# 64-row last terms of two tiles in the two halves of TensorE's rows

## The chip, the cores and the metric

The kernel runs on one core of a Trainium2 chip. The metric is the device time of one execution in microseconds (us), the median of several runs. Beside the runs there is one profiled execution, whose trace tells each instruction's start and length; its span is the time from its first to its last instruction.

## The reference

Sequence length S = 2048, width D = 576, 32 heads of 18, all in float32.

```
xn  = layernorm(x)
qkv = xn @ wqkv                       # [2048, 3*576]
# per head: a query at position p sees the 8 positions p, p-2, ..., p-14
o   = softmax(q . k[window] * 18**-0.5) . v[window]
h   = max(xn @ w1, 0)                 # [2048, 4608]
out = x + o @ wo + h @ w2
```

## The kernel before

**Split numbers.** Each float32 operand is kept as a high part rounded to float32r, which TensorE multiplies in one pass, and a low part, the rest. A product is the sum of high by high, low by high and high by low. The contraction of 576 is four blocks of 128 rows and one of 64 (`DR`). In xT, block 4 ("mix") holds the high part of these 64 rows in partitions 0 to 63 and the low part in partitions 64 to 127; in w1, wq and wo the 64 rows are loaded twice, into both halves. `TERMS` (line 307) lists the 14 matmuls of one product: four of high by high, four of x low by w high, `(4, 4)`, which does both for the last 64 rows at once, and five of x by w low. The last of these, `(4, 9)`, is the 64-row block by w low; all 128 rows go through it, though only the upper 64 are of use.

**Phases, slots, steps.** Positions are taken in two phases (even and odd ones); each has eight row tiles `i` of 128 positions, or four blocks `tb` of 256. A slot is one (phase, chunk, tb, f): one h tile of 128 hidden units by 256 positions. There are 2 x 12 x 4 x 3 = 288 slots, and chunk c covers hidden units f = 0, 1, 2. The main loop (line 680) takes one step `n` per slot, and the order in which it issues is the order of each engine's queue:

1. `run_splits(n)`: weights that are due are split: `two` (line 136) makes the high part on ACT (line 137) and the low part on DVE (line 141). w1 is due 5 steps and w2 3 steps ahead of its slot's number, wq in the five steps ahead of its unit.
2. `h_mm(n + 2)`: 14 matmuls into a bank of the pool `ps_h`, which has two; then `h_out`: relu to hhi on ACT (line 500), and hlo on DVE (line 503). The hlo is the last reader of the bank.
3. What `todo` holds: `qkv_tile`, `wo_f`, `wo_b`, x loads, `make_xt` (five transposes, lines 274 and 275, and the splits of xT on ACT and DVE).
4. `o_mm(n)`: 12 matmuls of h by w2 into `ps_o`; after each third slot (f = 2) two adds into x on DVE (line 544).
5. What `todo_late` holds: attention's start, norms, `wo_a`, `wo_s`; then `run_bg`: attention runs on DVE as a queue of small pieces (`qk_mul` line 358, `qk_sum` line 361, `av_mul` line 388, `av_add` line 395 and the softmax between them). A piece is issued while the kernel's own count of DVE time, `t["dve"]`, is at most its count of PE time, `t["pe"]`, plus a margin of 3.0, 1.5 or 3.0 us.

qkv is done in four units of 8 heads in each phase. A unit has eight tiles, one a step, each 14 matmuls of 128x432 into a bank of `ps_m` (two banks), and three copies out on ACT (lines 327 to 329). The units begin at steps 7, 34, 61 and 88 of a phase, and wo at 123. After the unit's last tile ACT issues the halo's DMAs (line 333).

Of the kernel before, what the change touches and what calls it, by code (L numbers as in the profile page):

```python
# [10 lines left out]
F32 = mybir.dt.float32  # L11
F32R = mybir.dt.float32r
AF = mybir.ActivationFunctionType
# [4 lines left out]
P = 128  # L18
NPH = 2
NI = 8  # L20
NTB = 4
TBN = 256
W = 8
HG = 8
NU = 4
# [1 line left out]
LAG = 2  # L27
EPS = 1e-5

UNIT0, UNIT_STEP, WO_AT = 7, 27, 8  # L30
WO_STEPS = (0, 1, 3, 4, 6, 7, 9, 10)
HEADW = (-9, -8, -7, -6, -5, -4)
FIRST = 4

HEAD = (
# [12 lines left out]
def tile_body(ctx: ExitStack, tc: tile.TileContext, x, wqkv, wo, w1, w2, out):  # L48
    nc = tc.nc
# [3 lines left out]
    UD = HG * Dh  # L53
# [3 lines left out]
    DR = D - KT * P  # L57
# [5 lines left out]
    ctx.enter_context(tc.manual_schedule())  # L63
    pool = lambda name, bufs, **k: ctx.enter_context(tc.tile_pool(name=name, bufs=bufs, **k))
    consts = pool("consts", 1)
    xp = pool("xp", 11)
    xtp = pool("xtp", NTB)
    qop = pool("qop", 1)
    kp = pool("kp", 1)
# [4 lines left out]
    stp = pool("stp", 5)  # L74
    hp = pool("hp", LAG + 2)
    prp = pool("prp", 2)
    lgp = pool("lgp", 2)
    smp = pool("smp", 2)
    tmp = pool("tmp", 2)
    turned = pool("turned", 3, space=bass.MemoryType.DRAM)  # L80
# [1 line left out]
    ps_h = pool("ps_h", 2, space=PSUM)  # L82
    ps_m = pool("ps_m", 2, space=PSUM)
# [18 lines left out]
    t = {"pe": 0.0, "dve": 0.0}  # L102

    def mm(o, l, r, start, stop, n):
        nc.tensor.matmul(o, l, r, start=start, stop=stop)  # L105
        t["pe"] += n / 2400.0 + 0.002
# [5 lines left out]
    tasks = deque()  # L112
    staged = deque()
# [19 lines left out]
    by_pool = set()  # L133
# [10 lines left out]
    W1, W2, WQ, WO = {}, {}, {}, {}  # L144
# [76 lines left out]
    X, XT, XN, MR = {}, {}, {}, {}  # L221
# [39 lines left out]
            dve(600)  # L261
        XN[ph, i] = xn

    def transpose_split(src, hi, mix, lo, bank=None, parts=False):

        if bank is ps_o:
            po = ps_o.tile([P, 2, 512], F32, name="po")
            pa, pb = po[:, 0, :].rearrange("p (k c) -> p k c", k=KT), po[0:DR, 1, 0:P]
        else:
            pa = ps_m.tile([P, KT, P], F32, name="pm")  # L270
            pb = ps_h.tile([P, TBN], F32, name="ph") if bank is ps_h else ps_m.tile([P, P], F32, name="pm")
            pb = pb[0:DR, 0:P]
        for k in range(KT):
            nc.tensor.transpose(pa[:, k, :], src[:, k * P : (k + 1) * P], ident)  # L274
        nc.tensor.transpose(pb, src[:, KT * P : D], ident)
        t["pe"] += 5 * 0.06

        def high():
            nc.scalar.activation(hi, pa, AF.Copy)  # L279

        def low():
            nc.vector.tensor_tensor(lo, pa, f32(hi), op=ALU.subtract)
            dve(512)

        def last_high():
            nc.scalar.activation(mix[0:DR], pb, AF.Copy)

        def last_low():
            nc.vector.tensor_tensor(mix[DR:P], pb, f32(mix[0:DR]), op=ALU.subtract)
            dve(128)  # L290

        steps = high, low, last_high, last_low
        if not parts:
            for f in steps:
                f()
        return steps

    def make_xt(ph, i, bank=None, parts=False):
        tb, h = divmod(i, 2)
        if h == 0:  # L300
            XT[ph, tb] = xtp.tile([P, 9, TBN], F32R, name="xT")
        d = XT[ph, tb][:, :, h * P : (h + 1) * P]
        xn = XN.pop((ph, i))
        return transpose_split(xn, d[:, 0:4, :], d[:, 4, :], d[:, 5:9, :], bank, parts)


    TERMS = [(k, k) for k in range(KT)] + [(5 + k, k) for k in range(KT)] + [(4, 4)] + [(k, 5 + k) for k in range(5)]


    QO, KK, VV = {}, {}, {}  # L310

    def qkv_tile(ph, u, i):
        if u == 0 and i == 0:
            QO[ph] = qop.tile([P, NI, D], F32, name="qo")
        if i == 0:
            assert len(bg) < 38, len(bg)
            KK[ph, u] = kp.tile([P, W - 1 + NI, UD], F32, name="k")
            VV[ph, u] = vp.tile([P, W - 1 + NI, UD], F32, name="v")
            nc.gpsimd.memset(KK[ph, u][0:1, 0 : W - 1, :], 0.0)
            nc.gpsimd.memset(VV[ph, u][0:1, 0 : W - 1, :], 0.0)  # L320
        k, v, wq = KK[ph, u], VV[ph, u], WQ[ph, u]
        tb, h = divmod(i, 2)
        xt = XT[ph, tb]
        pq = ps_m.tile([P, 3, UD], F32, name="pm")
        for j, (a, b) in enumerate(TERMS):
            mm(pq, xt[:, a, h * P : (h + 1) * P], wq[:, b, :], j == 0, j == len(TERMS) - 1, 3 * UD)
        nc.scalar.activation(k[:, W - 1 + i, :], pq[:, 1, :], AF.Copy)  # L327
        nc.scalar.activation(v[:, W - 1 + i, :], pq[:, 2, :], AF.Copy)
        nc.scalar.activation(QO[ph][:, i, u * UD : (u + 1) * UD], pq[:, 0, :], AF.Copy)
        if i == NI - 1:  # L330
            for z in (k, v):
                for a, b in HALO:
                    nc.scalar.dma_start(z[a + 1 : b + 1, 0 : W - 1, :], z[a:b, NI : NI + W - 1, :])

    bg = deque()
# [141 lines left out]
    slots = [(ph, c, tb, f) for ph in range(NPH) for c in range(NCH) for tb in range(NTB) for f in range(C)]  # L477
    H, PO = {}, {}

    HP, HN = {}, {}  # L480

    def h_terms(n, terms, other=False):
        ph, c, tb, f = slots[n]
        w, xt = W1[ph, c, f], XT[ph, tb]
        if n not in HP:
            HP[n] = ps_m.tile([P, TBN], F32, name="pm") if other else ps_h.tile([P, TBN], F32, name="ph")
            HN[n] = 0
        for a, b in terms:
            wb = w[:, b // 5, (b % 5) * P : (b % 5 + 1) * P]
            HN[n] += 1  # L490
            mm(HP[n], wb, xt[:, a, :], HN[n] == 1, HN[n] == len(TERMS), TBN)

    def h_out(n, parts=False):
        pt = HP.pop(n)
        hi = hp.tile([P, TBN], F32R, name="hhi")
        lo = hp.tile([P, TBN], F32R, name="hlo")
        H[n] = (hi, lo)

        def high():
            nc.scalar.activation(hi, pt, AF.Relu)  # L500

        def low():
            nc.vector.scalar_tensor_tensor(lo, pt, 0.0, f32(hi), op0=ALU.max, op1=ALU.subtract)  # L503
            t["dve"] = max(t["dve"], t["pe"] + 0.6)
            dve(TBN)

        if not parts:
            high()
            low()
        return high, low  # L510

    def h_mm(n):
        h_terms(n, TERMS)
        h_out(n)

    def o_mm(n, out=True):
# [39 lines left out]
    todo = {}  # L556

    def at(n, f, *a):
        todo.setdefault(n, []).append((f, a))

    todo_late = {}

    def late(n, f, *a):
        todo_late.setdefault(n, []).append((f, a))
# [2 lines left out]
    for ph in range(NPH):  # L567
        b = ph * SPP
        for c in range(NCH):
            for f in range(C):  # L570
                s = b + c * SPC + f
                first = ph == c == 0
                plan.append((HEADW[f] if first else s - 5, w1_task, ((ph, c, f), c * C + f)))
                plan.append((HEADW[3 + f] if first else s - 3, w2_task, ((ph, c, f), c * C + f)))
        for u in range(NU):
            s = b + UNIT0 + u * UNIT_STEP
            plan.append((s - 5, wq_tasks, ((ph, u), u)))
            for i in range(NI):
                at(s + i, qkv_tile, ph, u, i)
            late(s + NI + 1, attention, ph, u)  # L580
        s = b + UNIT0 + NU * UNIT_STEP + WO_AT
        plan.append((s - 8, wo_tasks, (ph,)))
        for i in range(NI):
            z = s + WO_STEPS[i]
            late(z, wo_a, ph, i)
            at(z + 1, wo_f, ph, i)
            late(z + 2, wo_s, ph, i)
            at(z + 3, wo_b, ph, i)
            at(z + 3, done, ph, i)
        if ph + 1 < NPH:  # L590
            e = b + SPP - SPC
            for i in range(NI):
                z = e + 3 + 2 * i
                at(z - 6, load_x, ph + 1, i)
                late(z - 2, stats, ph + 1, i)
                late(z - 1, norm, ph + 1, i)
                at(z + 1, make_xt, ph + 1, i)
# [4 lines left out]
            f(step, *a)  # L602
    tasks = deque(sorted(tasks, key=lambda z: z[0]))

    by_pool.update((-9, -8, *range(UNIT0 - 5, UNIT0)))
    both, x_low, w_low, last = TERMS[0:4], TERMS[4:8], TERMS[9:13], [TERMS[8], TERMS[13]]
    load_x(0, 0, 2)
    load_x(0, 1)
# [9 lines left out]
    x0 = make_xt(0, 0, parts=True)  # L618
    x0[0]()
    run_splits(-9)  # L620
    x1 = make_xt(0, 1, bank=ps_o, parts=True)
# [57 lines left out]
    M = (3.0, 1.5, 3.0)  # L679
    for n in range(FIRST, len(slots)):  # L680
        run_splits(n)
        m = n + LAG
        if m < len(slots):
            h_mm(m)
        for f, a in todo.pop(n, []):
            f(*a)
        if n >= 0:
            o_mm(n)
        for f, a in todo_late.pop(n, []):
            f(*a)  # L690
        run_bg(M[slots[n][3] if n >= 0 else 0])
    assert not todo and not todo_late and not bg and not tasks and not staged


# [24 lines left out]
```

## Time and profile before

| | |
|---|---|
| median of 3 runs | 1180.94 us (1180.86 to 1181.31) |
| the profiled execution | 1181.42 us, its span 1179.7 us |
| PE busy | 1171.0 us, 8936 matmuls |
| h matmuls (ph<-xT,w1t 128x256) | 4018 records, 278 ns mean length |
| o matmuls (po<-w2t, 128x288) | 3456, 293 to 296 ns |
| qkv matmuls (pm<-wq,xT 128x432) | 896, 358 ns |
| DVE busy | 818.8 us |
| hlo (line 503) | 287, 421 ns mean |
| ACT busy | 301.9 us |
| granted TensorE clock | 1.00 |

PE is the row of matmuls, PEld that of weight loads, which run ahead of their matmuls; a matmul's length in the table reaches past the start of the next one, so what counts for time is the distance between starts. DVE is VectorE, ACT ScalarE. A line of the timeline gives start and length in us, engine, line, operation, what it writes and reads, shapes and how many are merged, and in brackets how long the engine was idle before and what ended that.

### The profile page before, as it was taken

Reading aid. Unit: us, or ns where it says so; the run is one execution under the profiler, and the core shown is the slowest. Engines: PE = TensorE matmul, PEld = TensorE weight load, DVE = VectorE, ACT = ScalarE, POOL = GpSimd, SP = SyncE. Lnnn points to the kernel's source line nnn. Section 1 sums busy time; section 2 is a strip of 40 time slices with the busy share of each in tenths; the row PEclk is TensorE's granted clock in tenths of the full one; section 3 lists DMA queues with packets and bytes.
Section 4 is the critical chain, followed back from the end, with each engine's and each line's share of the span. In section 5 each row is a group of like instructions: output and inputs, shape, how many; then the busy total and the mean of one; then the engine's idle time right before and its main releaser. Section 6 shows DMA issues by size and latency. Waiting matters only on the chain.

```text
span 1179.7 us, 21695 instructions
## 1 busy us (share of the span) xinstructions
PE 1171.0 (99%) x8936; PEld 1162.3 (99%) x8936; DVE 818.8 (69%) x1298; ACT 301.9 (26%) x738; POOL 47.5 (4%) x70
## 2 busy tenths in 40 slices
PE   8999999999999999999999999999999999999998
PEld 8999999999999999999999999999999999999998
DVE  7427875888687678877673288758777884887752
ACT  5412222131222222321233123121222322222210
POOL 3200000010000000000020000000100000000000
PEclk9999999999999999999999999999999999999999
DMA  5312121130321211355342113030302313113431
GB/s 182 97 34 76 55 61 56 38 108 1 99 58 46 74 48 42 94 129 134 107 148 66 46 53 88 27 83 23 96 22 79 79 34 89 54 30 99 110 99 61
DMA packets 137650, 86.15 MB, mean 73 GB/s; under 512 B 48864, under 2 KB 121312, under 8 KB 137552
## 3 DMA queue, kind: packets, MB, share of 16 engines
q1 hardware_dynamic: 134736, 76.28, 23.7%
q10 hardware_dynamic: 2816, 8.49, 2.5%
q8 instruction: 70, 1.15, 0.4%
q14 instruction: 28, 0.23, 0.1%
HBM read 66.58 MB, written 9.96 MB: 65 GB/s over the span
## 4 chain that ended last, share of the span: by engine, by line
PE 96%; DVE 1%; DMA 1%; ACT 0%; issue 0%; POOL 0%; SPq 0%; DVEq 0%; ACTq 0%; POOLq 0%
PE ph L105 38%; PE po L105 38%; PE pm L105 20%; PE pm L274 0%; DVE bst L239 0%; DMA xn<-turned 0%; DMA x<-in_x 0%; DMA st<-in_wqkv 0%; DMA turned<-tr 0%; DVE pr L395 0%; POOL rstd L245 0%; DVE w2t L141 0%; ACT xn L257 0%; DVE hlo L503 0%; DVE x L550 0%
## 5 line engine op out<-in xcount | busy, mean ns | idle before, releaser
L105 PE MATMUL ph<-xT,w1t 128*128 128x256 f32 x4018 | 509.3, 278 | 0.7 <-ACT xT L279 0.7
L105 PEld LDWEIGHTS ph<-xT,w1t 128*128 128x128 f32 x4018 | 489.1, 188 | 1.1 <-ACT xT L279 1.0
L105 PE MATMUL po<-w2t,hhi 128*128 128x288 f32 x2304 | 400.7, 296 | 0.0
L105 PEld LDWEIGHTS po<-w2t,hhi 128*128 128x128 f32 x2304 | 337.0, 188 | 1.0
L500 ACT ACTIVATE hhi<-ph 128x256 fp32r<-128x256 f32 x287 | 109.9, 383 | 583.4 <-PE ph L105 560.2
L105 PE MATMUL po<-w2t,hlo 128*128 128x288 f32 x1152 | 245.0, 293 | 0.0
L503 DVE SCALAR_TENSOR_TENSOR hlo<-ph,hhi 128x256 fp32r<-128x256 f32 x287 | 120.8, 421 | 169.2 <-ACT hhi L500 168.5
L544 DVE TENSOR_TENSOR x<-po,x 128x576 f32<-128x576 f32 x190 | 142.5, 756 | 67.2 <-PE po L105 64.1
L105 PE MATMUL pm<-wq,xT 128*128 128x432 f32 x896 | 185.5, 358 | 0.0
L105 PEld LDWEIGHTS po<-w2t,hlo 128*128 128x128 f32 x1152 | 183.8, 188 | 0.0
L105 PEld LDWEIGHTS pm<-wq,xT 128*128 128x128 f32 x896 | 163.8, 188 | 5.6
L358 DVE TENSOR_TENSOR pr<-qo,k 128x1152 f32<-128x1152 f32 x64 | 85.8, 1348 | 0.0
L361 DVE TENSOR_REDUCE lg<-pr 128x64 f32<-128x1152 f32 x64 | 84.9, 1342 | 0.0
L388 DVE TENSOR_TENSOR pr<-lg,v 128x1152 f32<-128x1152 f32 x64 | 84.6, 1348 | 0.2
L141 DVE TENSOR_TENSOR w2t<-st,w2t 128x576 fp32r<-128x576 f32 x72 | 54.3, 754 | 40.4 <-ACT w2t L137 40.2
L395 DVE TENSOR_TENSOR pr<-pr 128x288 f32<-128x288 f32 (+1 forms) x128 | 70.4, 598 | 0.1
L141 DVE TENSOR_TENSOR w1t<-st,w1t 128x640 fp32r<-128x640 f32 x70 | 57.3, 818 | 12.1 <-ACT w1t L137 12.0
L137 ACT ACTIVATE w2t<-st 128x576 fp32r<-128x576 f32 x72 | 49.3, 685 | 55.1 <-PE po L105 46.5
L327 ACT ACTIVATE k<-pm 128x144 f32<-128x144 f32 x64 | 18.6, 291 | 146.5 <-PE pm L105 146.5
L137 ACT ACTIVATE w1t<-st 128x640 fp32r<-128x640 f32 x72 | 52.9, 735 | 2.5 <-DMA st<-in_w 2.3
L364 POOL TENSOR_SCALAR_AFFINE_SELECT lg<-lg 1x512 f32<-1x512 f32 x8 | 9.4, 1172 | 836.7 <-DVE lg L361 836.7
L105 PE MATMUL pm<-wq,oT 128*128 128x288 f32 x224 | 35.2, 296 | 0.8 <-ACT oT L451 0.8
(71 smaller groups left out, 444.2 us busy)
## 6 DMA issues: line engine op xcount, KB each, us to landing
st<-in_w SPq DMA_DIRECT2D x72, 288.0 KB, 3.0
st<-in_w SPq DMA_DIRECT2D x72, 256.0 KB, 3.1
st<-in_wqkv SPq DMA_DIRECT2D x32, 216.0 KB, 3.1
turned<-tr SPq DMA_DIRECT2D x64, 80.0 KB, 2.2
xn<-turned SPq DMA_DIRECT2D x16, 320.0 KB, 3.3
st<-in_w SPq DMA_DIRECT2D x144, 32.0 KB, 2.8
x<-in_x SPq DMA_DIRECT2D x15, 288.0 KB, 4.4
out<-x SPq DMA_DIRECT2D x14, 288.0 KB, 2.2
```

The costliest lines, as they stand in the source:

```text
L105: nc.tensor.matmul(o, l, r, start=start, stop=stop)
L137: nc.scalar.activation(hi, src, AF.Copy)
L141: nc.vector.tensor_tensor(lo, src, f32(hi), op=ALU.subtract)
L327: nc.scalar.activation(k[:, W - 1 + i, :], pq[:, 1, :], AF.Copy)
L358: nc.vector.tensor_tensor(pr[i], q, window(k, i), op=ALU.mult)
L361: nc.vector.tensor_reduce(lg[:, i], pr.pop(i).rearrange(heads, d=Dh), axis=AX.X, op=ALU.add)
L364: nc.gpsimd.affine_select(out=z, in_=z, pattern=[[1, NI], [1, W], [0, HG]], compare_op=ALU.is_ge, fill=-1e9 / scale, base=1 - W, channel_m ...
L388: nc.vector.tensor_tensor(pr[i].rearrange(heads, d=Dh), e, window(v, i).rearrange(heads, d=Dh), op=ALU.mult)
L395: nc.vector.tensor_tensor(o, z[:, 0:n], z[:, n : 2 * n], op=ALU.add)
L500: nc.scalar.activation(hi, pt, AF.Relu)
L503: nc.vector.scalar_tensor_tensor(lo, pt, 0.0, f32(hi), op0=ALU.max, op1=ALU.subtract)
L544: nc.vector.tensor_tensor(acc, PO[k][:, :, 0:D2], acc, op=ALU.add)
```

## The change

From step 8 on, at each even step `h_pair` issues the `(4, 9)` terms of the two next slots ahead of everything else of TensorE in that step. Each is a matmul of 64 rows: the first slot's reads partitions 0 to 63 of w1's low part and of mix, the second slot's partitions 64 to 127, where w1 has the same rows and where xT has a tenth block, the "twin", with the same high part. They open the two banks of `ps_h`, and each slot's other 13 terms add to them in its own step. Likewise `qkv_pair` opens the two banks of `ps_m` for two qkv tiles. The twin is one more copy on ACT for each row tile. Unit starts become even steps, the last x tile of the second phase is prepared a step earlier, and to make room `xp` has 10 buffers instead of 11 and `lgp` one instead of two; x loads for the second phase come 4 steps ahead instead of 6 from the third tile on.

```diff
-UNIT0, UNIT_STEP, WO_AT = 7, 27, 8
+UNITS, WO_AT = (8, 34, 62, 88), 123
+PAIRED = 8
...
-    xp = pool("xp", 11)
+    xp = pool("xp", 10)
-    lgp = pool("lgp", 2)
+    lgp = pool("lgp", 1)
...
         def last_high():
             nc.scalar.activation(mix[0:DR], pb, AF.Copy)
+            nc.scalar.activation(twin[DR:P], pb, AF.Copy)
...
-            XT[ph, tb] = xtp.tile([P, 9, TBN], F32R, name="xT")
+            XT[ph, tb] = xtp.tile([P, 10, TBN], F32R, name="xT")
...
+    def pair(o0, o1, x0, x1, w0, w1, n, weights_move):
+        for o, x, w, rows in ((o0, x0[0:DR, 4], w0[0:DR], 0), (o1, x1[DR:P, 9], w1[DR:P], 1)):
+            nc.tensor.matmul(o, *((x, w) if weights_move else (w, x)), start=True, stop=False)
+        t["pe"] += n / 2400.0 + 0.002
...
+    def qkv_pair(ph, u, i):
+        xt, w = XT[ph, i // 2], WQ[ph, u][:, 9, :]
+        a, b = PQ[i], PQ[i + 1] = [ps_m.tile([P, 3, UD], F32, name="pm") for _ in range(2)]
+        pair(a, b, xt[:, :, 0:P], xt[:, :, P:TBN], w, w, 3 * UD, True)
...
-        pq = ps_m.tile([P, 3, UD], F32, name="pm")
-        for j, (a, b) in enumerate(TERMS):
-            mm(pq, xt[:, a, h * P : (h + 1) * P], wq[:, b, :], j == 0, j == len(TERMS) - 1, 3 * UD)
+        pq = PQ.pop(i)
+        for a, b in TERMS[:-1]:
+            mm(pq, xt[:, a, h * P : (h + 1) * P], wq[:, b, :], False, (a, b) == TERMS[-2], 3 * UD)
...
+    def h_pair(n):
+        o, x, w = [], [], []
+        for m in (n, n + 1):
+            ph, c, tb, f = slots[m]
+            HP[m] = ps_h.tile([P, TBN], F32, name="ph")
+            HN[m] = 1
+            x.append(XT[ph, tb])
+            w.append(W1[ph, c, f][:, 1, 4 * P : 5 * P])
+            o.append(HP[m])
+        pair(*o, *x, *w, TBN, False)
...
     def h_mm(n):
-        h_terms(n, TERMS)
+        h_terms(n, TERMS[:-1] if n in HP else TERMS)
         h_out(n)
...
-            s = b + UNIT0 + u * UNIT_STEP
+            s = b + UNITS[u]
...
+                if i % 2 == 0:
+                    begin.setdefault(s + i, []).append((qkv_pair, (ph, u, i)))
...
-                at(z - 6, load_x, ph + 1, i)
+                at(z - (6 if i < 2 else 4), load_x, ph + 1, i)
+                z -= i == NI - 1
...
         m = n + LAG
         if m < len(slots):
+            if n >= PAIRED and n % 2 == 0:
+                h_pair(m)
+            for f, a in begin.pop(n, []):
+                f(*a)
             h_mm(m)
```

More of the change, by code (lines that the diff above doesn't have):

```diff
@@ L262, in norm, with transpose_split @@
         XN[ph, i] = xn
-    def transpose_split(src, hi, mix, lo, bank=None, parts=False):
+    def transpose_split(src, hi, mix, lo, twin, bank=None, parts=False):
         if bank is ps_o:
@@ L300, in make_xt @@
         if h == 0:
-            XT[ph, tb] = xtp.tile([P, 9, TBN], F32R, name="xT")
+            XT[ph, tb] = xtp.tile([P, 10, TBN], F32R, name="xT")
         d = XT[ph, tb][:, :, h * P : (h + 1) * P]
         xn = XN.pop((ph, i))
-        return transpose_split(xn, d[:, 0:4, :], d[:, 4, :], d[:, 5:9, :], bank, parts)
+        return transpose_split(xn, d[:, 0:4, :], d[:, 4, :], d[:, 5:9, :], d[:, 9, :], bank, parts)
     TERMS = [(k, k) for k in range(KT)] + [(5 + k, k) for k in range(KT)] + [(4, 4)] + [(k, 5 + k) for k in range(5)]
+    def pair(o0, o1, x0, x1, w0, w1, n, weights_move):
+        for o, x, w, rows in ((o0, x0[0:DR, 4], w0[0:DR], 0), (o1, x1[DR:P, 9], w1[DR:P], 1)):
+            nc.tensor.matmul(o, *((x, w) if weights_move else (w, x)), start=True, stop=False)
+        t["pe"] += n / 2400.0 + 0.002
     QO, KK, VV = {}, {}, {}
+    PQ = {}
+    def qkv_pair(ph, u, i):
+        xt, w = XT[ph, i // 2], WQ[ph, u][:, 9, :]
+        a, b = PQ[i], PQ[i + 1] = [ps_m.tile([P, 3, UD], F32, name="pm") for _ in range(2)]
+        pair(a, b, xt[:, :, 0:P], xt[:, :, P:TBN], w, w, 3 * UD, True)
     def qkv_tile(ph, u, i):
@@ L559, in at @@
         todo.setdefault(n, []).append((f, a))
-    todo_late = {}
+    todo_late, begin = {}, {}
     def late(n, f, *a):
@@ L575, in tile_body @@
         for u in range(NU):
-            s = b + UNIT0 + u * UNIT_STEP
+            s = b + UNITS[u]
             plan.append((s - 5, wq_tasks, ((ph, u), u)))
             for i in range(NI):
+                if i % 2 == 0:
+                    begin.setdefault(s + i, []).append((qkv_pair, (ph, u, i)))
                 at(s + i, qkv_tile, ph, u, i)
             late(s + NI + 1, attention, ph, u)
-        s = b + UNIT0 + NU * UNIT_STEP + WO_AT
+        s = b + WO_AT
         plan.append((s - 8, wo_tasks, (ph,)))
@@ L603, in tile_body @@
     tasks = deque(sorted(tasks, key=lambda z: z[0]))
-    by_pool.update((-9, -8, *range(UNIT0 - 5, UNIT0)))
+    by_pool.update((-9, -8, *range(UNITS[0] - 5, UNITS[0])))
     both, x_low, w_low, last = TERMS[0:4], TERMS[4:8], TERMS[9:13], [TERMS[8], TERMS[13]]
@@ L691, in tile_body @@
         run_bg(M[slots[n][3] if n >= 0 else 0])
-    assert not todo and not todo_late and not bg and not tasks and not staged
+    assert not begin and not todo and not todo_late and not bg and not tasks and not staged
 def kernel(**inputs):
```

## The prediction

> **What bounds the kernel now.** I read the page first: busy shares, then the chain that ended last.
>
> ```profile
> PE 1171.0 (99%) x8936; PEld 1162.3 (99%) x8936; DVE 818.8 (69%) x1298; ACT 301.9 (26%) x738; POOL 47.5 (4%) x70
> ...
> PE 96%; DVE 1%; DMA 1%; ACT 0%; issue 0%; POOL 0%; SPq 0%; DVEq 0%; ACTq 0%; POOLq 0%
> ```
>
> TensorE is the bound: the chain is 96% PE. Every matmul taken off shortens the end, and every wait put in front of PE lengthens it, one for one. DVE at 69% looks like slack, so I asked the view of waits how VectorE stands to PE at the one instruction that frees an h bank, the hlo of line 503.
>
> ```profile
> DVE hlo L503 <- ACT hhi L500: 168.5, 135, 5.5
> ```
>
> There are 288 hlo, and DVE waited for the relu (hhi) before 135 of them. The others began when DVE was done with older work: DVE is behind there. Today that costs nothing, since ps_h has two banks and a tile's bank is wanted again only two slots on. How late it is I read from the timeline, here slot 48's start (adds, attention, splits, hlo of slot 47):
>
> ```profile
> 204.24 1.55 DVE L544 TENSOR_TENSOR x<-po,x 128x576 f32<-128x576 f32 x2
> ...
> 205.71 1.35 DVE L358 TENSOR_TENSOR pr<-qo,k 128x1152 f32<-128x1152 f32 x1
> ...
> 206.64 0.38 ACT L500 ACTIVATE hhi<-ph 128x256 fp32r<-128x256 f32 x1 [1.62 <-PE ph L105]
> ...
> 206.97 0.75 DVE L141 TENSOR_TENSOR w2t<-st,w2t 128x576 fp32r<-128x576 f32 x1
> ...
> 207.64 0.82 DVE L141 TENSOR_TENSOR w1t<-st,w1t 128x640 fp32r<-128x640 f32 x1
> ...
> 208.03 0.98 PE L105 MATMUL ph<-xT,w1t 128*128 128x256 f32 x7
> ...
> 208.38 0.42 DVE L503 SCALAR_TENSOR_TENSOR hlo<-ph,hhi 128x256 fp32r<-128x256 f32 x1
> ```
>
> Slot 48's matmuls start at 208.03, and slot 47's hlo ends at 208.79, 0.76 us later. The relu was done at 207.02; the two weight splits and an attention piece stood ahead on DVE.
>
> **Part 1: matmuls taken away.** Starts in the trace give the cadence: h 113 to 119 ns a matmul (14 in 1.61 us), o 132, qkv 196. The change pairs slots 10 to 287, 139 pairs, and 64 qkv tiles, 32 pairs. Each pair swaps two full matmuls for two of 64 rows; if these ran as one, h would save 139 x 0.11 = 15.3 us and qkv 32 x 0.19 = 6.1 us, 21.4 us in all. The other end is nothing saved. No row has two matmuls side by side, but one shows what a weight load costs by itself, a matmul that PE had to wait for:
>
> ```profile
> 1093.20 0.19 PEld L105 LDWEIGHTS pm<-wq,oT 128*128 128x128 f32 x1 [1.03 <-ACT oT L451]
> 1093.20 0.41 PE L105 MATMUL pm<-wq,oT 128*128 128x288 f32 x1 [0.83 <-ACT oT L451]
> ```
>
> It took 0.41 us where its like take 0.29 to 0.30, and its successor began 241 ns after it instead of 132. So a load of 128 columns is 0.107 us, hidden only under the matmul before it, and h's 113 ns is just that. A pair still has two such loads, and nothing in the trace shows two loads at once. I take loads one after another, matmuls side by side. With 0 at the end of the last o matmul, the first load has 132 to hide in and is done at -25, the second at 82, the next full matmul's at 189, which then starts at about 195: 33 ns saved of 228. With a qkv pair behind, loads end at 82, 189 and 296, and the last qkv matmul ends at 296 + 196 = 492 against 620: 128 ns saved. 107 x 0.033 + 32 x 0.128 = 7.6 us.
>
> **Part 2: going into half rows and back.** 139 bursts, 278 changes. The nearest row is the 64-column transpose of line 275 among full matmuls: from its start to the second full matmul behind it 229 ns passed, where 109 + 118 = 227 would at an even cadence; with an o matmul behind it, 4 or 5 ns were lost. Its 16 cases would make 278 x 2 to 5 ns, 1.0 us. Below nothing it cannot be. The other end is under C.
>
> **Part 3: the new wait.** The pair at an even step opens both banks, so its second matmul needs the hlo of the slot just before, which PE used to need one slot later. PE's order of the changed program has that wait: the second matmul of line 315 waits for DVE. Behind it in PE's queue stands everything: thirteen terms of the slot, qkv, and o, so nothing covers it. I measured at every even slot of the trace, as above, how long after its first matmul the hlo before it ended. In the first half (us): 24: 0.76, 34: 1.91, 36: 2.64, 48: 0.76, 60: 1.27, 84: 0.76, 88: 1.13, 90: 1.25, 96: 1.01, 108: 0.76, 116: 0.29, 118: 1.01, 120: 0.83, 144: 0.62, together 15.0. The second half repeats them without the last, 14.4. I leave out 18, 72 and 216 (0.24, 1.59, 1.60): there the relu was late behind the halo's DMAs on ACT, and units now end at odd steps, so the late relu belongs to an even slot. All 27 waits in full: 29.4 us; if one wait in a cluster (34/36, 88/90, 116 to 120) absorbs the next, 21.1. Each wait also exposes a load, 0.107, and the hand-over, 0.03: 2.7 to 3.8. Low end 24, high end 33, and up to 3 more because PE arrives sooner where pairs save. I take 30. A cluster pays more than its maximum: ahead of slot 35's hlo stand two adds (0.76), the maximum (1.16), and wq, w2t and w1t splits (0.60, 0.75, 0.82), with the hlo 5.3 us less 0.08 for each overlap, against some 4.0 us that PE has from when the first add can start; a second wait of about 1 us survives one at 34.
>
> The qkv pair opens both pm banks and needs wq's last split at once. The banks: three copies on ACT (0.29, 0.29, 0.30) after the last tile lie under the 1.59 us of o matmuls; without that cover 0.9 us a pair. The split stands on DVE ahead of the odd hlo that the h pair has just waited for: no wait of its own.
>
> The order of DVE's queue in the changed program keeps this: ahead of slot 47's hlo it has the same adds, piece and splits.
>
> **Part 4: the rest.** The twin copies are 16 more activations like line 286's, 0.26 us each, on an engine at 26%; only the first two lie on the start: 0.3 us. One lg buffer costs nothing, as DVE works its units in order. Ten x buffers make the third x load wait for an output (2.2 us to landing) and then 4.4 us, under more than two steps of 3.2: nothing; without that cover, about 1 us once. No DMA is added; units and the last xT a step apart from before put no work on PE.
>
> **Sum.** +30 - 7.6 + 1.0 + 0.3 = +23.7 us. The profiled execution was 1181.42 us (span 1179.7), 0.5 over the median of 1180.94; on the median, 1204.6. Its own range, with waits from 24 to 36 and pairs saving 9 to nothing: 1196 to 1218.
>
> **The rivals.**
>
> A, the sum above: 0.42.
>
> B, the halves run side by side, loads too. For it: nothing in the order forbids it, and the two write different banks. Against: the 0.107 us loads never overlap in this trace. Gain 21.4, waits 33 as PE comes sooner: +12, about 1193 (1184 to 1196). [...] 0.23.
>
> C, each change of form empties the array. Then the next load isn't hidden (0.107) and, at worst, the last matmul runs out first: it took 276 ns at a cadence of 113, another 0.163. 278 times 0.107 to 0.27 is 30 to 75 us. Less 21.4 plus 30 of waits: 1219 to 1265, likelier at the low end, 1230, as line 275's row shows nothing of it. That row speaks against C, but it cuts columns, not rows. [...] 0.30.
>
> D, the other side: not slower. run_bg gives DVE as much as PE's estimate allows, and that now falls by 0.109 us a pair; where an attention piece of 1.35 us slips behind the odd hlo, a wait of 0.76 to 1.27 is gone. It decides where waits fall under the gain: below 21.4 in B's case, so a third or more of the 27 places must clear. With half cleared, 14 - 21.4 = -7, 1174. Against it: the order holds as many pieces there as before. 0.05.
>
> **Numbers.** A measurement of this kernel can tell about 0.2%, 2.4 us, from no change. Only D gains that much, 0.04; its rest and B's edge lie within it, 0.02; slower 0.94. The range runs from 1190 (B's middle and up) to 1240 (C's low half); outside lie D, B's low tail and C's high part, about 0.18.
>
> **What would show it.** Right: PE idle of some 30 us in front of ph at line 315, ended by DVE hlo, about once in each twelve slots and more where splits of wq fall; idle of PE elsewhere as before; DVE's busy time unchanged. For A, the pair's second matmul about 0.1 us after the first; for B, a few ns; for C, a gap of 0.1 us or more on both sides of each pair. Wrong: no idle at line 315 (D), or PE's stretches without waits longer than before (C).

## The result, and the profile after

The changed kernel takes 1246.33 us (1244.82 to 1247.52, four runs) against 1180.90: a ratio of 1.0553, interval [1.0534, 1.0571], 65 us slower. The forecast was slower, 1204.6, with a range to 1240; the time lies 6 us above it.

The page of the kernel after, busy shares and the chain that ended last:

```profile
span 1244.5 us, 21715 instructions
...
PE 1217.8 (98%) x8936; PEld 1160.5 (93%) x8936; DVE 821.0 (66%) x1297; ACT 307.2 (25%) x754; POOL 50.0 (4%) x71
...
PE 82%; DVE 10%; issue 3%; DMA 2%; ACT 1%; SPq 1%; POOL 0%; DVEq 0%; ACTq 0%; POOLq 0%
```

DVE has come into the chain with 10% (1% before), and "issue", time in which an engine waits for nothing that the profile shows, with 3%. DVE's own busy time is what it was (818.8 before). The view of waits, lines of the pairs alone (us in total, times, longest):

```profile
PEld ph L315 <- DVE hlo L529: 25.2, 38, 1.6
PEld ph L315 <- issue: 20.7, 127, 0.2
...
PE ph L315 <- DVE hlo L529: 18.0, 28, 1.4
```

Two different things stand in front of line 315: a few long waits for hlo, and 127 short ones, 0.16 us each, that no semaphore ends. The timeline around one pair without a wait for hlo:

```profile
235.68 0.43 PE L106 MATMUL po<-w2t,hlo 128*128 128x288 f32 x2
236.03 0.19 PEld L315 LDWEIGHTS ph<-xT,w1t 64*128 64x128 f32 x2 [0.16 <-issue]
236.04 0.38 PE L315 MATMUL ph<-xT,w1t 64*128 64x256 f32 x2
236.35 0.54 PEld L106 LDWEIGHTS ph<-xT,w1t 128*128 128x128 f32 x4
236.35 0.62 PE L106 MATMUL ph<-xT,w1t 128*128 128x256 f32 x3
```

The two halves and their two loads start together (236.04 for both; 3 ns apart in the records). But the last o matmul began at 235.81, and the loads of the halves only at 236.03, 0.22 us later, where a load otherwise starts 3 ns after the matmul before it. On the other side the next full load waits until 236.35. So at each change of form no load runs ahead of its matmul, and PE stands for about 0.09 us besides: in front 0.22 us pass between the starts instead of 0.13, and behind 0.31, where an exposed load (0.107) and a matmul (0.113) make 0.22.

Call the half-row matmuls that follow one another without a full one between them a burst. Taken over all 139 bursts, from the start of the last o matmul to that of the second full h matmul, against the cadence of before: 283 ns more for a burst with an h pair alone, 80 more with a qkv pair behind it, 107 x 0.283 + 32 x 0.080 = 33 us. On top, the second half started late in 33 bursts, 28.9 us in all. Here is the one at slot 48, whose lateness the prediction had shown:

```profile
214.79 0.82 DVE L142 TENSOR_TENSOR w1t<-st,w1t 128x640 fp32r<-128x640 f32 x1
...
215.16 0.38 PE L315 MATMUL ph<-xT,w1t 64*128 64x256 f32 x1
...
215.53 0.42 DVE L529 SCALAR_TENSOR_TENSOR hlo<-ph,hhi 128x256 fp32r<-128x256 f32 x1
...
216.00 0.38 PE L315 MATMUL ph<-xT,w1t 64*128 64x256 f32 x1 [0.46 <-DVE hlo L529]
```

The first half goes at 215.16, the second when hlo has ended, at 216.00: 0.84 us. Together 62 of the 64.8 us by which the span has grown. Of the rest, 1.7 us is a stretch at a clock of 0.50 (last section), and 0.6 us falls behind the last matmul. What is left, about 1 us, fits what lies further behind the bursts with a qkv pair: over two whole steps such a burst costs 0.11 to 0.18 us more than before, not 0.08. Why is open.

### The profile page after: what moved, and what is told of

It reads as the page before. It is cut to its first block, busy times and chain, and to the rows that moved or that the text cites. A ratio compares the mean times of both kernels' runs of the same rounds, so it can differ in the third digit from the quotient of the medians.

```text
span 1244.5 us, 21715 instructions
## 1 busy us (share of the span) xinstructions
PE 1217.8 (98%) x8936; PEld 1160.5 (93%) x8936; DVE 821.0 (66%) x1297; ACT 307.2 (25%) x754; POOL 50.0 (4%) x71
## 4 chain that ended last, share of the span: by engine, by line
PE 82%; DVE 10%; issue 3%; DMA 2%; ACT 1%; SPq 1%; POOL 0%; DVEq 0%; ACTq 0%; POOLq 0%
PE ph L106 31%; PE po L106 30%; PE pm L106 17%; PE ph L315 3%; DMA st<-in_w 2%; DVE lg L376 1%; DVE w1t L142 1%; DVE w2t L142 1%; DVE hlo L529 1%; DVE pr L373 1%; DVE m L385 1%; PE pm L315 1%; DVE wq L142 0%; DVE x L570 0%; DVE pr L403 0%
## 5 line engine op out<-in xcount | busy, mean ns | idle before, releaser
L106 PE MATMUL ph<-xT,w1t 128*128 128x256 f32 x3740 | 493.6, 282 | 0.7 <-ACT xT L280 0.7
L106 PEld LDWEIGHTS ph<-xT,w1t 128*128 128x128 f32 x3740 | 455.2, 188 | 21.7 <-issue 6.8
L106 PE MATMUL pm<-wq,xT 128*128 128x432 f32 x832 | 174.4, 360 | 0.0
L106 PEld LDWEIGHTS pm<-wq,xT 128*128 128x128 f32 x832 | 152.7, 189 | 5.5
L315 PE MATMUL ph<-xT,w1t 64*128 64x256 f32 x278 | 64.4, 381 | 18.0 <-DVE hlo L529 18.0
L315 PEld LDWEIGHTS ph<-xT,w1t 64*128 64x128 f32 x278 | 31.2, 183 | 46.2 <-DVE hlo L529 25.2
```

The lines of the kernel that those rows point to most:

```text
L315: nc.tensor.matmul(o, *((x, w) if weights_move else (w, x)), start=True, stop=False)
```

## The experiments

Theory T: each change between full and half rows has a price (a load that cannot be hidden, 0.107 us, and 0.09 us for which PE stands, as around the pair above), the halves themselves run side by side (3 ns between their starts), and the waits for hlo, 28.9 us, come on top.

**Waits without half rows.** The order is kept; both matmuls of a pair go through all rows.

```diff
-((o0, x0[0:DR, 4], w0[0:DR], 0), (o1, x1[DR:P, 9], w1[DR:P], 1))
+((o0, x0[:, 4], w0, 0), (o1, x1[:, 4], w1, 1))
```

> The changed kernel with its order kept, but both matmuls of a pair go through all 128 rows, as the term did before; no half-row form is left. Theory T: the loss has two parts, about 29 us of waits for the odd hlo in front of the pairs, and a price for every change between full and half rows (0.107 us of exposed weight load and 0.09 us of running empty); then only the waits are left: 1208 to 1214 us, and 220 to 230 ns from pair to next full matmul vanish. Rival R1: the time around the pairs is lost by the order itself (PE's queue held at the pair, banks opened early), not by the form: 1235 to 1250.

Measured 1216.57 us, ratio 1.0299 [1.0269, 1.0329]: 35.3 us more than before, 2.6 us above the expected range and far from R1. The timeline of slot 48:

```profile
212.00 0.42 PE L106 MATMUL po<-w2t,hlo 128*128 128x288 f32 x2
212.26 0.28 PE L315 MATMUL ph<-xT,w1t 128*128 128x256 f32 x1
213.19 0.39 PE L315 MATMUL ph<-xT,w1t 128*128 128x256 f32 x1 [0.65 <-DVE hlo L529]
213.41 0.75 PE L106 MATMUL ph<-xT,w1t 128*128 128x256 f32 x5
```

The pair's first matmul follows o at the old distance, and the second's wait is there. 34 bursts lost 34.0 us, the other 105 together 0.6. They lose more than in the changed kernel (28.9) mostly because each wait also exposes a load (3.6 us), which there is already counted with the change of form; the lateness alone is 30.4 us.

**Half rows without pairs or waits.** The kernel before; in `h_terms`:

```diff
+            r = 64 if (a, b) == TERMS[-1] else P
-            mm(HP[n], wb, xt[:, a, :], HN[n] == 1, HN[n] == len(TERMS), TBN)
+            mm(HP[n], wb[0:r], xt[0:r, a, :], HN[n] == 1, HN[n] == len(TERMS), TBN)
```

> The kernel before, with one edit: the last term of each h tile takes 64 rows (upper half) in its old place, 288 lone half-row matmuls, no pair and no early bank. T: two changes of form each, 2 x 0.198 us, nothing saved: 288 x 0.396 = 114 us, 1290 to 1298, and no wait for hlo. R1: the form costs nothing, 1179 to 1184.

Measured 1291.94 us, ratio 1.0937 [1.0905, 1.0969]: 110.7 us over before, 0.384 us for each of 288. It is the price of the form alone, two changes each: 0.19 us a change. The by-form view of PEld has the part that stands in front (the last number is PEld's idle time before):

```profile
L105 PEld LDWEIGHTS ph<-xT,w1t 64*128 64x128 f32 x287 | 52.5, 183 | 36.3
```

That two matmuls add to the same bank is not what costs. In this run the half writes the bank of the matmul before it (206 ns between the starts instead of 113), and the matmul behind it writes another bank (310 ns, and 239 instead of 133 to the next). In the changed kernel it is the other way round, with much the same losses (225 instead of 131 in front, 311 and 222 behind).

**The same with 96 rows** (`r = 96` above).

> The kernel before with 96 rows in the last term of each h tile. [...] Rival R2, fewer rows as such cost: near the 64-row run, 1270 to 1298.

Measured 1185.64 us, ratio 1.0037 [1.0021, 1.0053]. R2 is out: 96 rows cost 4 us where 64 cost 111. But T, which puts the price on the half-row form, had 1180 to 1183, as before, and that does not hold either: the matmul of 96 rows has its successor after 120 ns instead of 113, and small shifts follow in o and qkv, 15 ns each in all. Why is open.

**The pair one after the other.** Both halves are the upper one.

```diff
-(o1, x1[DR:P, 9], w1[DR:P], 1)
+(o1, x1[0:DR, 4], w1[0:DR], 1)
```

> The changed kernel, but both matmuls of a pair use the upper half (the high part is there too), one after the other in the same form. T, halves and their loads at once: the second now costs a matmul more, 0.113 us for 139 h pairs and 0.196 for 32 qkv pairs, 22 us less what falls under the waits of 33 pairs: 1264 to 1270. Rival R3, the 3 ns between the starts are only how the record is made and halves run one after the other anyway: 1243 to 1249.

Measured 1265.79 us, ratio 1.0715 [1.0684, 1.0747], 19.5 us over the changed kernel: as T had it. The second half now starts 0.22 us after the first instead of 3 ns, and the next full load comes 0.43 us after the first half's, where it is 0.31 to 0.32 in the changed kernel:

```profile
91.84 0.29 PEld L315 LDWEIGHTS ph<-xT,w1t 64*128 64x128 f32 x2 [0.16 <-issue]
91.84 0.50 PE L315 MATMUL ph<-xT,w1t 64*128 64x256 f32 x2
92.27 0.76 PEld L106 LDWEIGHTS ph<-xT,w1t 128*128 128x128 f32 x6
```

So the gain of the change is real: a pair on two halves saves the length of one matmul against two on the same half.

**Pairs at odd steps.** `UNITS = (7, 35, 63, 89)`, `PAIRED = 9`, and

```diff
-            if n >= PAIRED and n % 2 == 0:
+            if n >= PAIRED and n % 2 == 1 and m + 1 < len(slots):
```

> The changed kernel with the pairs, and the units of qkv, at odd steps (pairs of slots 11 and 12, 13 and 14, ...): the pair then needs the hlo of an even slot, which stands on DVE ahead of the two splits of a chunk's end instead of behind them. T: the price of the changes of form stays (33 us with 139 bursts), the waits fall from 28.9 to 6 to 11 us: 1222 to 1230. Rival R4, DVE is late as a whole, and the waits only go to other slots: 1240 to 1248.

Measured 1221.12 us, ratio 1.0338 [1.0317, 1.0358], 25 us less than the changed kernel. The view of waits:

```profile
PEld ph L315 <- issue: 21.0, 129, 0.2
PEld ph L315 <- DVE hlo L529: 6.2, 9, 1.4
PE ph L315 <- DVE hlo L529: 4.6, 4, 1.2
```

The 129 short stops are as they were; the long ones fell to 6.4 us of late second halves, in 8 bursts. R4 is out: DVE isn't late as a whole, but mostly at the odd slots, where the splits of a chunk's end stand ahead. Nearly all that is left are four waits of 1.5 to 1.6 us at the start of units of qkv. What this kernel takes more than the one before, 39.9 us, is 33.0 of changes, 6.4 of waits and half a us.

**h pairs alone**, at even steps; `qkv_tile` with its 14 terms as before, no `qkv_pair`.

> The changed kernel with h pairs at even steps, but every qkv tile with its 14 full matmuls: 64 half-row matmuls fewer. T, a price per burst (two changes) and a gain per pair: all 139 bursts now cost 0.283 us, 39 us, and waits of 28 to 33: 1250 to 1257, slower than the changed kernel. Rival R5, a price per half-row matmul: 278 of 342, so 27 us instead of 33: 1236 to 1242.

Measured 1249.59 us, ratio 1.0579 [1.0558, 1.06]: 64 half-row matmuls fewer, and slower than the changed kernel. It is 0.4 us under T's range and clear of R5's. From the trace: 139 x 0.283 = 39.3 of changes and 27.8 of waits, 67.2 of the span's 67.6 us. The price goes by bursts.

**qkv pairs alone, and four in a burst.** Both at odd steps: `PAIRED = 999`, and in the second run

```diff
-            if n >= PAIRED and n % 2 == 1 and m + 1 < len(slots):
+            if n >= PAIRED and n % 2 == 1 and n in begin:
```

> Pairs of qkv alone, at odd steps, h with its 14 full matmuls: 32 bursts of two. T: 0.396 less 0.196 a burst, 6.4 us, and waits for wq's last split and the copies, at most 5: 1186 to 1193. R5: 64 of 342 half-row matmuls, 6 us: the same, told apart by the next run.

> As the run with qkv pairs alone, and an h pair only in front of a qkv pair: 32 bursts of four half-row matmuls. T: 0.080 us a burst, 2.6 us, less than with two in a burst, and waits of 2 to 7 for hlo: 1185 to 1191. R5: 128 of 342 half-row matmuls, 12 us and the same waits: 1195 to 1200. Faster than before would need over 0.396 us saved in a burst, and four save 0.309.

Measured 1194.18 us, ratio 1.0109 [1.0092, 1.0126], and 1198.93, 1.0145 [1.0129, 1.016]. Both lie above T's ranges, and the second's total is where R5 had it. Their traces give the parts. A burst of four without a wait:

```profile
51.60 0.43 PE L106 MATMUL po<-w2t,hlo 128*128 128x288 f32 x2
51.97 0.39 PE L315 MATMUL ph<-xT,w1t 64*128 64x256 f32 x2
52.19 0.36 PE L315 MATMUL pm<-wq,xT 64*128 64x432 f32 x2
52.47 0.50 PE L106 MATMUL ph<-xT,w1t 128*128 128x256 f32 x2
```

Counted around the burst, as in the changed kernel, one with two half-row matmuls costs 189 ns (27 of the 32), and one with four 79 to 92: 0.200 and 0.080 us were T's figures. Over two whole steps it is 0.22 us with two and 0.11 to 0.18 with four. Either way the price falls with more halves in a burst, where R5 needs it to double. What T had too low is this remainder behind the burst (some 1 to 2 us in all) and the waits: 5.1 us in the first run, just over the 5 allowed, and 7.9 in the second, where four pairs waited 1.8 to 2.0 us. Three of these were followed by 3.4 us at a clock of 0.50, 1.7 us lost each. So the total can't tell T from R5 here; the price per burst can.

**A cut of the columns.** The kernel before, in `h_terms`:

```diff
+            c = DR if (a, b) == TERMS[-2] else P
-            mm(HP[n], wb, xt[:, a, :], HN[n] == 1, HN[n] == len(TERMS), TBN)
+            mm(HP[n][0:c], wb[:, 0:c], xt[:, a, :], HN[n] == 1, HN[n] == len(TERMS), TBN)
```

> The kernel before; the last but one term of each h tile (the fourth block by w low) is made for the first 64 hidden units of the tile alone, so it has 128 rows and 64 columns; the product for the other 64 hidden units is left out. It asks why the row of line 275 showed no price. T', only a cut of the rows has the price, a cut of the columns none: 1176 to 1184. Rival R6, any change of form has it, and line 275 hides it because transposes run otherwise: 288 x 0.38, near 1290.

Measured 1181.25 us, ratio 1.0000 [0.9989, 1.0012]. The form is there, 64 columns wide, and PEld never idles before its load, where it idled 36.3 us before the 287 loads of 64 rows:

```profile
L105 PE MATMUL ph<-xT,w1t 128*64 128x256 f32 x287 | 79.2, 276 | 0.0
...
L105 PEld LDWEIGHTS ph<-xT,w1t 128*64 128x64 f32 x287 | 38.5, 134 | 0.0
```

R6 is out: a cut of the columns costs nothing, a cut to half the rows 0.384 us.

**The price at a longer matmul.** The kernel before, 64 rows in the last term of each qkv tile.

> The kernel before with 64 rows in the last term of each of the 64 qkv tiles, in its old place. T, the price of the two changes is the same for a matmul of 432 as for one of 256 columns, 0.384 us as measured for h: 64 x 0.384 = 24.6 us, 1203 to 1208. Rival R7, the price is a share of the matmul's length (0.384 of 0.113 us, 3.4 times): 64 x 0.66 = 42 us, 1220 to 1226.

Measured 1207.16 us, ratio 1.022 [1.0191, 1.025]: 25.8 us, 0.40 us each, as T has it; R7 is out.

## Why the prediction was right or wrong

*Direction, and the wait.* Right in the main. The hlo of the odd slot came into the chain, at most of the slots that were read from the trace of before: 24 with 0.82 us (0.76 forecast), 48 with 0.84 (0.76), 60 with 1.34 (1.27), 108 with 0.83 (0.76). The first half of the run lost 14.5 us, where the list gave 15.0 at full price. That the sums agree so closely is in part luck. 34 and 36 lost 1.30 and 1.13 instead of 1.91 and 2.64 (probably since the first wait lets DVE catch up), 88 lost nothing instead of 1.13, and 64, 134 and 150 came in that the list did not have. At 64 and 90, and again at 208 and 234, 6.7 us in all, DVE was late not only with older work: DVE and ACT waited for each other. The softmax's exp on ACT (line 389) waited for DVE, and then what stands ahead of the hlo on DVE waited for ACT, at 64 a sum for the exp (0.76 us), at 90 the low part of wq for the high part, which ACT made behind the exp (1.21 us). Slot 90:

```profile
380.36 0.69 DVE L388 TENSOR_TENSOR lg<-lg,m 128x512 f32<-128x512 f32 x1
...
381.15 0.63 ACT L389 ACTIVATE lg<-lg 128x512 f32<-128x512 f32 x1 [3.83 <-DVE lg L388]
...
381.69 0.55 ACT L138 ACTIVATE wq<-st 128x432 fp32r<-128x432 f32 x1
382.14 0.36 ACT L526 ACTIVATE hhi<-ph 128x256 fp32r<-128x256 f32 x1
382.26 0.61 DVE L142 TENSOR_TENSOR wq<-st,wq 128x432 fp32r<-128x432 f32 x1 [1.21 <-ACT wq L138]
382.79 0.42 DVE L529 SCALAR_TENSOR_TENSOR hlo<-ph,hhi 128x256 fp32r<-128x256 f32 x1
...
383.26 0.38 PE L315 MATMUL ph<-xT,w1t 64*128 64x256 f32 x1 [1.38 <-DVE hlo L529]
```

The 30 us that were taken came out as 28.9, but the 30 held exposed loads (0.107 us a wait, some 3 us) that the 28.9 do not. The run at odd steps shows that it was the wait for hlo: it took 22 us of it away by letting the pair need another hlo.

*Part 2, the changes of form.* Here the forecast failed. It priced 278 changes at 1.0 us, by the transpose of line 275, the nearest row in the trace. That row cuts the columns; the change cuts the rows. The column run fits the reading of that row, and shows that a cut of columns says nothing of rows; the lone halves show what rows cost, 0.19 us a change, and 278 x 0.19 = 53 us stand where 1.0 stood. I had named the objection ("it cuts columns, not rows") and still taken its value for the sum.

*Part 1, the halves.* The forecast took loads one after another, for 7.6 us saved. They run side by side (3 ns apart), so a pair saves a whole matmul, about 21 us in all, as under B; the run in the same half confirms it (19.5 us, as some of the 21 falls under waits). This error, 14 us, was in the other direction and hid about a quarter of the first: 53 - 21 = 32, where the traces have 33 and the forecast had 1.0 - 7.6.

*The rivals.* C was the case, with 0.30, and its price lay between its bounds (0.107 and 0.27 a change; measured 0.19). Its value of 1230 leaned to the low end for line 275's sake, the same wrong row again; the middle of its bounds is 1242, 4 us under what was measured. The lone halves have that price, 0.384 us for two changes; the 64 columns, at 1181.25 us against 1181.36, have none. That the array empties was my assumption: what the traces show is a load that does not run ahead (0.107 us) and PE standing for 0.09 us besides. B's half, that both matmuls run at once and their loads too, came as well: 3 ns lie between the starts, and two matmuls on the same half took 19.5 us more. So the signs named for B (a few ns) and for C (a gap on both sides) both came: two cases that I had set against each other both held.

*Range and chances.* 1240 cut C near the middle of its 1219 to 1265, though C had 0.30 and only 0.18 in all was thought to lie outside the range. Slower at 0.94 was right.

*Part 4.* Right within a few tenths. Up to the first unit of qkv PE stands 0.2 us ahead of the kernel before, so the 0.3 us of the first twin copies do not show; the 0.6 us behind the last matmul were not foreseen.

## What to carry to other kernels

A half-row matmul among full ones pays for its surroundings: here 0.38 to 0.40 us for going in and out, against 0.11 to 0.20 us that a second half saves. It can pay only where a burst saves more than that; h and qkv pairs together save 0.309, and no burst tried here got there.

An operation moved ahead needs its buffer earlier too: before opening a bank a slot sooner, read from the trace how late its last reader is at each slot. An engine at 69% was behind at 27 places by the trace of before, and 33 pairs waited. And where a cost is bounded from a near row, the forecast should not stand at that row if what it lacks is just the property that the change has.

## What the runs showed of the hardware

Among full float32r matmuls, as the three such runs on the kernel before show, a cut to 64 of 128 rows costs 0.19 us a change (1291.94 us against 1181.26), a cut to 64 of 128 columns nothing (1181.25 against 1181.36), and a matmul of 96 rows 15 ns (1185.64 against 1181.26).

The granted clock fell after some waits of 1.75 to 2.0 us. In the kernel after, the second half of a pair waited 1.75 us until 999.99, and soon after it PE ran at a clock of 0.50 for 3.4 us. The view of stretches (length, busy times with instruction counts, then the granted clock, DMA share, GB/s), that one and one before it:

```profile
1001.30:1004.60 3.30, 3.30 (x14) 3.18 (x13) 1.29 (x3) 0.38 (x1) 0.00 (x0) 0.50 0.19 69
990.30:993.60 3.30, 3.30 (x27) 3.01 (x26) 2.20 (x3) 0.61 (x2) 1.29 (x2) 1.00 0.38 102
```

14 matmuls instead of 27, at a clock of 0.50. The run in the same half had one such stretch, after a wait of 1.78 us, and the run with four in a burst three, each after a wait of 1.8 to 2.0 us; of its four runs, the three with a mean clock of 0.995 took 1198.4 to 1199.9 us, the one with 0.999 took 1195.6. The length of the wait alone doesn't decide it: the kernel after waited just as long at slot 90 (1.76 us), and the run of waits with full rows up to 1.9 us, and no such stretch followed. What decides it is open.
